# Ten weight buffers instead of two, six output buffers instead of two, three-fold buffers between the engines of the output stage, and ScalarE's output copy one step later

## The chip, the cores and the metric

The kernel runs on one core of one Trainium2 chip. The metric is device time in microseconds (us), lower is better. In this kernel each engine runs its own program, in which it waits for semaphores that the others raise: TensorE (matmul and transpose, with results in the memory called PSUM), VectorE, ScalarE, and the DMA queues, mostly fed by the Sync engine. In the views of the profile PE is TensorE, PEld its weight loads, DVE VectorE, ACT ScalarE and POOL GpSimd; L306 is line 306 of the kernel. "Landing" is the moment at which a DMA's data have arrived.

## The reference, cut to what matters

```python
# x: (8, 5696, 128) f32, h: (5696, 128); D = 128 channels, S = 5696 positions, batch 8
y = irfft(rfft(x, 2*S) * rfft(h, 2*S))[:, :S]         # causal long convolution, per channel
Y = rfft(y)[:, :64]                                    # the first 64 modes
Y = Y_r@w_r - Y_i@w_i + 1j*(Y_r@w_i + Y_i@w_r)         # per mode a 128 x 128 complex mix
u = y + irfft(Y)
out = u + maximum(u @ w_ch, 0)
```

w_r and w_i are 64 x 128 x 128 f32 each, 8.4 MB together; the output is 23.3 MB.

## The kernel before

The kernel works in stages: h and x are transposed and cast; then the *channel loop* multiplies, for each of 128 channels, a Toeplitz band (1440 KB, loaded as G[i], four buffers) by x; then a forward DFT on TensorE (90 matmuls), VectorE's two copies of its result out of PSUM (called XM), the mix, an inverse transform folded into the *output stage*. Two parts matter here.

The weight load. Sixteen chunks of 512 KB (8 modes each), preceded by the small w_ch (chunk 0), come in f32 through two staging buffers and are cast to f16 in turn by VectorE (even chunks) and ScalarE (odd ones):

```python
# Sync engine, after the channel loop's loads (cut)
for k, (kind, c) in enumerate(wchunks_s):
    if k >= NWST:                                   # NWST = 2
        sp.wait_ge(s_wc, k - NWST + 1)              # the chunk two before has been cast
    sp.dma_start(WST[k % NWST] ..., wsrc).then_inc(s_wl[k % NWST], 16)
# VectorE (even k) and ScalarE (odd k)
    wait_ge(s_wl[k % NWST], 16 * (k // NWST + 1)); wait_ge(s_wc, k)
    copy(wdst[:, m0 * D:(m0 + WMB) * D], WST[k % NWST][:, 0:WMB * D]).then_inc(s_wc, 1)
```

The output stage. It has 90 groups of four 128 x 128 tiles. For each group g: A (TensorE, 8 matmuls: u transposed, in PSUM), e1 (ScalarE copies it to uT), B (TensorE, u @ w_ch), d1 (VectorE: max and add, into oT), C (TensorE, 4 transposes back), e2 (the copy into the f32 output buffer ost, VectorE for even g and ScalarE for odd g), then the output DMA.

```python
# TensorE
for step in range(NG + 2):                          # NG = 90
    if step < NG:              stageA(step)
    if 1 <= step <= NG:        stageB(step - 1)
    if 2 <= step <= NG + 1:    stageC(step - 2)
# ScalarE
def emit_e2_act(gg):
    uu = gg % 2
    act.wait_ge(s_po, gg + 1)                       # C(gg) is done
    if gg >= 2:
        act.wait_ge(s_od[uu], 16 * (gg // 2))       # the DMA out of this ost has landed
    act.copy(ost[uu][:, :], pb16[6 + uu][:, 0:GB * P]).then_inc(s_e2a, 1)
for g in range(NG + 1):
    if g < NG:
        ...                                         # waits
        act.copy(uT_sb[ui][:, :], pb[2 + ui][:, 0:GB * P]).then_inc(s_e1, 1)
    if g >= 1 and (g - 1) % 2 == 1:
        emit_e2_act(g - 1)
# VectorE: d1(g), then e2(g-1) if g-1 is even
```

Of the kernel before, what the change touches and what calls it, by code (L numbers as in the profile page):

```python
# [4 lines left out]
P = 128  # L5
DT16 = mybir.dt.float16
DT32 = mybir.dt.float32
# [5 lines left out]
def bass_long_conv_fft__then__afno_spectral_mix_kernel(  # L13
    nc, x, h, moe_w_r, moe_w_i, moe_w_ch, out
):
    B, S, D = x.shape
# [12 lines left out]
    NGB = 4  # L29
    GB = min(4, B)  # L30
# [14 lines left out]
    WMB = 1  # L45
# [5 lines left out]
    NWLD_BASES = 1  # L51
    NWC_TOTAL = 1 + 2 * NWCH

    i16_np = np.eye(P, dtype=np.float16)
# [6 lines left out]
    for m in range(M):  # L61
# [19 lines left out]
    g_bytes = GC * 2  # L81
    ph2_bytes = (2 * HALF + B * P * 3 + 512 * 2) * 2 + 2 * GB * P * 2 * 2 + 2 * GB * P * 4
    xst_bytes = B * D * 4
# [18 lines left out]
    uT_sb = [nc.alloc_sbuf_tensor_at(f"uT_sb{i}", [P, GB * P], DT16, offset=p2 + i * GB * P * 2)  # L102
             for i in range(2)]
    p2 += 2 * GB * P * 2
    oT_sb = [nc.alloc_sbuf_tensor_at(f"oT_sb{i}", [P, GB * P], DT16, offset=p2 + i * GB * P * 2)
             for i in range(2)]
    p2 += 2 * GB * P * 2
    ost = [nc.alloc_sbuf_tensor_at(f"ost{i}", [P, GB * P], DT32, offset=p2 + i * GB * P * 4)
           for i in range(2)]
    p2 += 2 * GB * P * 4  # L110
    assert p2 <= r2_addr + r2_bytes, (p2 - r2_addr, r2_bytes)
# [16 lines left out]
    WST = [nc.alloc_sbuf_tensor_at(f"WST{i}", [P, WMB * D], DT32, offset=ib_addr + i * wst_bytes)  # L128
           for i in range(NWST)]
    WCH16 = nc.alloc_sbuf_tensor("WCH16", [P, D], DT16)  # L130
    I16 = nc.alloc_sbuf_tensor("I16", [P, P], DT16)
# [3 lines left out]
    pb = [nc.alloc_psum_tensor(f"pb{i}", [P, 512], DT32) for i in range(8)]  # L135
    pb16 = [pb[i][:, :].bitcast(DT16) for i in range(8)]

    def sem(name):
        return nc.alloc_semaphore(name)
# [16 lines left out]
    s_wld = sem("s_wld")  # L156
    s_wl = [sem("s_wl0"), sem("s_wl1")]
    s_wc = sem("s_wc")
# [15 lines left out]
    s_e2a = sem("s_e2a")  # L174
    s_od = [sem("s_od0"), sem("s_od1")]

    with nc.Block() as block:
        @block.sync
        def _(sp):
# [36 lines left out]
            for k, (kind, c) in enumerate(wchunks_s):  # L216
                if k >= NWST:
                    sp.wait_ge(s_wc, k - NWST + 1)
                if kind == "wch":
                    sp.dma_start(WST[k % NWST][:, 0:D], moe_w_ch).then_inc(s_wl[k % NWST], 16)  # L220
                else:
                    w = moe_w_r if kind == "wr" else moe_w_i
                    m0 = c * WMB
                    wsrc = bass.AP(w.tensor, w.offset + m0 * D * D, [[D, P], [D * D, WMB], [1, D]])
                    wdstap = bass.AP(WST[k % NWST], 0, [[WMB * D, P], [D, WMB], [1, D]])
                    sp.dma_start(wdstap, wsrc).then_inc(s_wl[k % NWST], 16)
            for g in range(NG):
                q = g // NGRP_Q
                b0 = (g % NGRP_Q) * GB
                rows = P if q < NQ - 1 else TAIL  # L230
                if g % 2 == 0:
                    sp.wait_ge(s_e2d, g // 2 + 1)
                else:
                    sp.wait_ge(s_e2a, (g - 1) // 2 + 1)
                osrc = bass.AP(ost[g % 2], 0, [[GB * P, rows], [P, GB], [1, P]])
                odst = bass.AP(out.tensor, out.offset + b0 * S * D + q * P * D,
                               [[D, rows], [S * D, GB], [1, D]])
                sp.dma_start(odst, osrc).then_inc(s_od[g % 2], 16)
            sp.wait_ge(s_od[0], 16 * ((NG + 1) // 2))
            if NG >= 2:  # L240
                sp.wait_ge(s_od[1], 16 * (NG // 2))

# [15 lines left out]
        def _(act):  # L258
# [31 lines left out]
            for k, (kind, c) in enumerate(wchunks_a):  # L290
                if k % 2 != 1:
                    continue
                act.wait_ge(s_wl[k % NWST], 16 * (k // NWST + 1))
                act.wait_ge(s_wc, k)
                wdst = WR16 if kind == "wr" else WI16
                m0 = c * WMB
                act.copy(wdst[:, m0 * D:(m0 + WMB) * D], WST[k % NWST][:, 0:WMB * D]).then_inc(s_wc, 1)  # L297
            act.wait_ge(s_xtp, B)
            act.wait_ge(s_xt, 1)
            act.activation(XTn_sb[:, :], pb16[6][:, 0:B * P], ACT_COPY, scale=-1.0).then_inc(s_xt, 1)  # L300
            def emit_e2_act(gg):
                uu = gg % 2
                act.wait_ge(s_po, gg + 1)
                if gg >= 2:
                    act.wait_ge(s_od[uu], 16 * (gg // 2))
                act.copy(ost[uu][:, :], pb16[6 + uu][:, 0:GB * P]).then_inc(s_e2a, 1)  # L306
            for g in range(NG + 1):
                if g < NG:
                    ui = g % 2
                    act.wait_ge(s_put, g + 1)  # L310
                    if g >= 2:
                        act.wait_ge(s_prt, g - 1)
                        act.wait_ge(s_d1, g - 1)
                    act.copy(uT_sb[ui][:, :], pb[2 + ui][:, 0:GB * P]).then_inc(s_e1, 1)  # L314
                if g >= 1 and (g - 1) % 2 == 1:
                    emit_e2_act(g - 1)

        @block.vector
        def _(dve):
# [28 lines left out]
            for k, (kind, c) in enumerate(wchunks):  # L348
                if k % 2 != 0:
                    continue  # L350
                dve.wait_ge(s_wl[k % NWST], 16 * (k // NWST + 1))
                if k >= 1:
                    dve.wait_ge(s_wc, k)
                if kind == "wch":
                    dve.tensor_copy(WCH16[:, :], WST[k % NWST][:, 0:D]).then_inc(s_wc, 1)  # L355
                else:
                    wdst = WR16 if kind == "wr" else WI16
                    m0 = c * WMB
                    dve.tensor_copy(wdst[:, m0 * D:(m0 + WMB) * D], WST[k % NWST][:, 0:WMB * D]).then_inc(s_wc, 1)  # L359
            dve.wait_ge(s_dft, 2)  # L360
# [16 lines left out]
            def emit_e2_dve(gg):  # L377
                uu = gg % 2
                dve.wait_ge(s_po, gg + 1)
                if gg >= 2:  # L380
                    dve.wait_ge(s_od[uu], 16 * (gg // 2))
                dve.tensor_copy(ost[uu][:, :], pb16[6 + uu][:, 0:GB * P]).then_inc(s_e2d, 1)  # L382
            for g in range(NG + 1):
                if g < NG:
                    ui = g % 2
                    dve.wait_ge(s_prt, g + 1)
                    dve.wait_ge(s_e1, g + 1)
                    if g >= 2:
                        dve.wait_ge(s_po, g - 1)
                    dve.scalar_tensor_tensor(oT_sb[ui][:, :], pb[4 + ui][:, 0:GB * P], 0.0,  # L390
                                             uT_sb[ui][:, :], MAXOP, ADDOP).then_inc(s_d1, 1)
                if g >= 1 and (g - 1) % 2 == 0:
                    emit_e2_dve(g - 1)

        @block.tensor
        def _(pe):
# [75 lines left out]
            def stageA(g):  # L472
                ui = g % 2
                q = g // NGRP_Q
                b0 = (g % NGRP_Q) * GB
                if g >= 2:
                    pe.wait_ge(s_e1, g - 1)
                last = None
                for j in range(GB):
                    b = b0 + j  # L480
                    ao = bass.AP(AXC, q * B + b, [[NTOT, P], [NCOL, P]])
                    cols = pb[2 + ui][:, j * P:(j + 1) * P]
                    pe.matmul(cols, ao, I16[:, :], start=True, stop=False)  # L483
                    last = pe.matmul(cols, C_sb[:, b * P:(b + 1) * P], IB_sb[:, q * P:(q + 1) * P],  # L484
                                     start=False, stop=True)
                last.then_inc(s_put, 1)

            def stageB(g):
                ui = g % 2
                if g >= 2:  # L490
                    pe.wait_ge(s_d1, g - 1)
                pe.wait_ge(s_e1, g + 1)
                pe.matmul(pb[4 + ui][:, 0:GB * P], WCH16[:, :], uT_sb[ui][:, :],  # L493
                          start=True, stop=True).then_inc(s_prt, 1)

            def stageC(g):
                ui = g % 2
                if g >= 2:
                    if g % 2 == 0:
                        pe.wait_ge(s_e2d, (g - 2) // 2 + 1)  # L500
                    else:
                        pe.wait_ge(s_e2a, (g - 3) // 2 + 1)
                pe.wait_ge(s_d1, g + 1)
                last = None
                for j in range(GB):
                    last = pe.transpose(pb16[6 + ui][:, j * P:(j + 1) * P],  # L506
                                        oT_sb[ui][:, j * P:(j + 1) * P], I16[:, :])
                last.then_inc(s_po, 1)
# [38 lines left out]
```

## Time and profile before

828.48 us, the median of 4 runs (827.27 to 829.39). The first rows of the page's picture of the span, in 40 slices of about 20.7 us, each digit the busy tenths of a slice, with the clock granted to TensorE below:

```profile
PE   0777775899999999999999999999997076666674
...
DVE  0555553011111111111111111111111235655564
...
PEclk9755555899999999999999999999999559999997
```

TensorE is full through the long middle (the channel loop and the DFT). Then comes one slice at 0, and after it a last part where nothing is full. The windows view of the kernel before puts numbers on it. Its columns are the stretch, its length, the busy us of TensorE, its weight loads, VectorE, ScalarE and GpSimd, the granted clock, the busy share of the DMA engines and GB/s:

```profile
148.00:600.00 452.00, 451.88 (x5566) 391.28 (x5567) 65.49 (x123) 0.00 (x0) 0.00 (x0) 0.99 1.00 406
...
616.00:635.00 19.00, 19.00 (x90) 8.61 (x88) 2.08 (x3) 4.10 (x4) 0.00 (x0) 1.00 0.69 193
636.00:656.00 20.00, 0.00 (x0) 0.00 (x0) 2.63 (x4) 4.18 (x4) 0.00 (x0) 0.54 0.72 204
...
690.00:740.00 50.00, 32.90 (x413) 25.35 (x411) 30.62 (x48) 23.46 (x46) 0.00 (x0) 1.00 0.57 165
```

From 636 to 656 TensorE does nothing. In the output stage (690 to 740) TensorE is busy 66%, VectorE 61%, ScalarE 47%, DMA 0.57. The chain of waits (the chain of work that ended last, in order of time: start, length, what) tells what each stretch waits for. First in the weight load:

```profile
615.86 4.33 DMA WST<-in_moe_w_r_dram
620.22 0.70 DVE WR L359
620.94 4.38 DMA WST<-in_moe_w_r_dram
625.35 0.70 DVE WR L359
...
```

A landing, a cast, a landing: with two buffers, the next load of a buffer starts only after its cast. The copies of XM stand behind the casts in VectorE's program, so TensorE's next work waits for the last cast (656.29). Then in the output stage, in the same view:

```profile
740.01 0.59 ACT ost L306
...
740.62 2.58 DMA out_dram<-ost
...
743.27 0.59 ACT ost L306
...
743.88 2.46 DMA out_dram<-ost
...
```

ScalarE's copy into its one ost buffer, the DMA out of it until it has landed, the next copy: once per pair of groups. The waits view of 690 to 740 us (engine and line, what it waited for, us in total, times, longest) names the same wait first:

```profile
ACT ost L306 <- DMA out_dram<-ost: 25.1, 15, 2.1
DVE oT_sb L390 <- PE pb L493: 20.3, 16, 1.7
PE pb L493 <- ACT uT_sb L314: 18.1, 16, 1.6
```

### The profile page before, as it was taken

The numbers are of one execution on the slowest core, as the hardware profiler recorded it, in microseconds if no ns is written. First come the engines' busy times: TensorE is split into PE (matmuls) and PEld (weight loads), VectorE is DVE, ScalarE is ACT, GpSimd is POOL, SyncE is SP. The second block draws the span as 40 slices with busy tenths as digits, with TensorE's granted clock in tenths as the row PEclk, the third lists the DMA queues.
The fourth block names the chain that finished last, engine by engine and source line by source line (L and its number), as shares of the span: only waits on it lengthen the run. The fifth ranks groups of instructions, "written<-read, shape, count | busy, mean of one in ns | idle before, by whom it ended". The sixth has DMA issues, their size and how long they took to land.

```text
span 827.0 us, 16480 instructions
## 1 busy us (share of the span) xinstructions
PE 689.0 (83%) x7435; PEld 514.3 (62%) x7435; DVE 232.3 (28%) x395; ACT 113.7 (14%) x213; POOL 2.5 (0%) x9
## 2 busy tenths in 40 slices
PE   0777775899999999999999999999997076666674
PEld 0200000688888888888888888888873064545453
DVE  0555553011111111111111111111111235655564
ACT  1322221000000000000000000000002215454443
POOL 0000000000000000000000000000000000000000
PEclk9755555899999999999999999999999559999997
DMA  9877774999999999999999999999956615555554
GB/s 264 228 211 222 218 216 156 367 393 419 401 418 400 409 409 410 403 407 406 413 404 411 407 406 411 404 414 399 416 215 193 193 54 163 169 156 172 156 156 141
DMA packets 130949, 252.43 MB, mean 305 GB/s; under 512 B 4864, under 2 KB 112704, under 8 KB 114112
## 3 DMA queue, kind: packets, MB, share of 16 engines
q1 hardware_dynamic: 121232, 152.55, 53.2%
q10 hardware_dynamic: 9360, 95.88, 28.6%
q0 software_dynamic: 288, 2.95, 1.0%
q8 instruction: 59, 0.97, 0.4%
q14 instruction: 10, 0.08, 0.0%
HBM read 226.53 MB, written 24.84 MB: 304 GB/s over the span
## 4 chain that ended last, share of the span: by engine, by line
PE 66%; DMA 21%; DVE 5%; issue 4%; ACT 3%; SPq 0%; ACTq 0%; DVEq 0%
PE pb L431 56%; DMA out_dram<-ost 13%; PE pb L419 6%; DVE X L335 4%; ACT ost L306 3%; DMA WST<-in_moe_w_r_dram 2%; DMA WST<-in_moe_w_i_dram 2%; DMA hnat<-in_h_dram 2%; PE pb L406 1%; DMA G<-hT16scr 1%; DMA hT16scr<-hTsb 1%; PE pb L493 0%; DVE WR L359 0%; DVE WI L359 0%; PE pb L483 0%
## 5 line engine op out<-in xcount | busy, mean ns | idle before, releaser
L431 PE MATMUL pb<-AXC,G 128*128 128x360 f16 (+44 forms) x5760 | 467.0, 243 | 9.2 <-DMA G<-hT16scr 9.2
L431 PEld LDWEIGHTS pb<-AXC,G 128*128 128x128 f16 x5760 | 404.4, 98 | 73.4 <-issue 10.8
L346 DVE CAST AXC<-pb 128x360 f16<-128x360 f32 x128 | 68.2, 532 | 408.8 <-PE pb L431 408.8
L419 PE MATMUL pb<-X,J 128*128 128x512 f16 x90 | 84.7, 1029 | 26.5 <-DVE X L335 23.4
L390 DVE SCALAR_TENSOR_TENSOR oT_sb<-pb,uT_sb 128x512 f16<-128x512 f32 x90 | 61.8, 686 | 58.3 <-PE pb L493 58.3
L493 PE MATMUL pb<-uT_sb,WCH 128*128 128x512 f16 x90 | 35.5, 395 | 50.0 <-ACT uT_sb L314 50.0
L419 PEld LDWEIGHTS pb<-X,J 128*128 128x128 f16 x90 | 9.2, 103 | 100.5 <-DVE X L335 93.0
L297 ACT CAST WR<-WST 128x1024 f16<-128x1024 f32 x4 | 4.2, 1045 | 490.2 <-DVE WCH L355 476.4
L483 PE MATMUL pb<-I,AXC 128*128 128x128 f16 x360 | 53.9, 230 | 2.6 <-DVE C_sb L376 2.6
L484 PE MATMUL pb<-IB_sb,C_sb 128*128 128x128 f16 x360 | 53.5, 226 | 0.0
L314 ACT CAST uT_sb<-pb 128x512 f16<-128x512 f32 x90 | 48.9, 598 | 14.5 <-PE pb L484 14.5
L483 PEld LDWEIGHTS pb<-I,AXC 128*128 128x128 f16 x360 | 44.9, 141 | 2.8 <-DVE C_sb L376 2.8
L342 DVE CAST AXC<-pb 128x512 f16<-128x512 f32 x45 | 31.1, 692 | 52.9 <-PE pb L419 52.9
L493 PEld LDWEIGHTS pb<-uT_sb,WCH 128*128 128x128 f16 x90 | 8.9, 99 | 56.6 <-DVE oT_sb L390 49.3
L484 PEld LDWEIGHTS pb<-IB_sb,C_sb 128*128 128x128 f16 x360 | 38.0, 106 | 0.3 <-issue 0.3
L277 ACT CAST AXC<-pb 128x512 f16<-128x512 f32 x45 | 26.3, 585 | 85.2 <-PE pb L419 78.8
L306 ACT CAST ost<-pb 128x512 f32<-128x512 f16 x45 | 26.3, 585 | 77.7 <-DMA out_dram<-ost 69.6
L506 PE MATMUL pb<-I,oT_sb 128*128 128x128 f16 x360 | 36.0, 224 | 0.4 <-DVE oT_sb L390 0.4
L506 PEld LDWEIGHTS pb<-I,oT_sb 128*128 128x128 f16 x360 | 25.3, 99 | 16.2 <-issue 13.5
L382 DVE CAST ost<-pb 128x512 f32<-128x512 f16 x45 | 31.0, 689 | 3.5 <-DMA out_dram<-ost 2.8
L335 DVE CAST X<-XST 128x1024 f16<-128x1024 f32 x45 | 30.7, 683 | 0.0
L406 PE MATMUL pb<-I,hnat 128*128 128x128 f32 (+1 forms) x45 | 9.0, 358 | 18.7 <-DMA hnat<-in_h_dram 18.7
(45 smaller groups left out, 129.7 us busy)
## 6 DMA issues: line engine op xcount, KB each, us to landing
G<-hT16scr SPq DMA_DIRECT2D x64, 1440.0 KB, 9.0
G<-hT16scr ACTq DMA_DIRECT2D x64, 1440.0 KB, 8.9
XST<-in_x_dram SPq DMA_DIRECT2D x44, 512.0 KB, 4.6
out_dram<-ost SPq DMA_DIRECT2D x88, 256.0 KB, 2.4
WST<-in_moe_w_r_dram SPq DMA_DIRECT2D x8, 512.0 KB, 4.5
WST<-in_moe_w_i_dram SPq DMA_DIRECT2D x8, 512.0 KB, 4.2
hT16scr<-hTsb ACTq DMA_DIRECT2D x1, 1472.0 KB, 6.4
FB_sb<-cFB POOLq DMA_DIRECT2D x1, 1440.0 KB, 6.8
```

The source lines that it names most:

```text
L306: act.copy(ost[uu][:, :], pb16[6 + uu][:, 0:GB * P]).then_inc(s_e2a, 1)
L314: act.copy(uT_sb[ui][:, :], pb[2 + ui][:, 0:GB * P]).then_inc(s_e1, 1)
L335: dve.tensor_copy(X16[qi][:, :], XST[qi][:, :]).then_inc(s_cast, 1)
L342: dve.tensor_copy(dst, pb[g % 2][:, 0:HCOLS]).then_inc(s_jevd, 1)
L346: dve.tensor_copy(AXC[:, d * NCOL:(d + 1) * NCOL], pb[d % 4][:, 0:NCOL]).then_inc(s_cev, 1)
L390: dve.scalar_tensor_tensor(oT_sb[ui][:, :], pb[4 + ui][:, 0:GB * P], 0.0, uT_sb[ui][:, :], MAXOP, ADDOP).then_inc(s_d1, 1)
L419: pe.matmul(pb[g % 2][:, 0:HCOLS], J16[:, :], moving, start=True, stop=True).then_inc(s_j, 1)
L431: ins = pe.matmul(pb[d % 4][:, B * l:NCOL], G[i][:, l * P:(l + 1) * P], AXC[:, d * NCOL:d * NCOL + ncols], start=(l == 0), stop=(l == NQ - 1))
L483: pe.matmul(cols, ao, I16[:, :], start=True, stop=False)
L484: last = pe.matmul(cols, C_sb[:, b * P:(b + 1) * P], IB_sb[:, q * P:(q + 1) * P], start=False, stop=True)
L493: pe.matmul(pb[4 + ui][:, 0:GB * P], WCH16[:, :], uT_sb[ui][:, :], start=True, stop=True).then_inc(s_prt, 1)
L506: last = pe.transpose(pb16[6 + ui][:, j * P:(j + 1) * P], oT_sb[ui][:, j * P:(j + 1) * P], I16[:, :])
```

## The change

The intent is to hide the weight load and to keep the output stage from waiting for its own output. Chunks 2 to 9 get buffers in the channel loop's G buffers, free as the last four channels finish. The output stage gets six ost buffers (NO) and three of uT, oT and their PSUM banks (ND). ScalarE's ost copy moves one step later in its program. The diff, cut to its core:

```diff
+    ND = 3
+    NO = 6
@@ weight staging
+    # chunk buffers 2..9: two in each G buffer, free once the last channel of that buffer is done
+    WST += [nc.alloc_sbuf_tensor_at(f"WSTG{i}", [P, WMB * D], DT32,
+                                    offset=r2_addr + (i // 2) * g_bytes + (i % 2) * wst_bytes)
+            for i in range(2 * NGB)]
+    NWB = len(WST)
@@ Sync engine
-                if k >= NWST:
-                    sp.wait_ge(s_wc, k - NWST + 1)
+                if k >= NWB:
+                    sp.wait_ge(s_wc, k - NWB + 1)
+                elif k >= NWST:
+                    sp.wait_ge(s_cd, D - NGB + 1 + (k - NWST) // 2)
@@ ScalarE
             def emit_e2_act(gg):
-                uu = gg % 2
+                uu = gg % NO
                 act.wait_ge(s_po, gg + 1)
-                if gg >= 2:
-                    act.wait_ge(s_od[uu], 16 * (gg // 2))
+                if gg >= NO:
+                    act.wait_ge(s_od[uu], 16 * (gg // NO))
-            for g in range(NG + 1):
+            for g in range(NG + 2):
                 if g < NG:
-                    ui = g % 2
+                    ui = g % ND
...
-                if g >= 1 and (g - 1) % 2 == 1:
-                    emit_e2_act(g - 1)
+                if g >= 2 and (g - 2) % 2 == 1:
+                    emit_e2_act(g - 2)
```

Left out: the same renaming of indices (2 to ND, NO or NWB) on the other engines; one added wait of VectorE for the last weight cast, because the buffers that follow lie over the new staging; and a constant that nothing uses.

More of the change, by code (lines that the diff above doesn't have):

```diff
@@ L52, in bass_long_conv_fft__then__afno_spectral_mix_kernel @@
     NWC_TOTAL = 1 + 2 * NWCH
+    WLOAD_START_D = max(NGB, D - 4 * (NWC_TOTAL + 3))
     i16_np = np.eye(P, dtype=np.float16)
@@ L81, in bass_long_conv_fft__then__afno_spectral_mix_kernel @@
     g_bytes = GC * 2
-    ph2_bytes = (2 * HALF + B * P * 3 + 512 * 2) * 2 + 2 * GB * P * 2 * 2 + 2 * GB * P * 4
+    ND = 3
+    NO = 6
+    ph2_bytes = (2 * HALF + B * P * 3 + 512 * 2) * 2 + 2 * ND * GB * P * 2 + NO * GB * P * 4
     xst_bytes = B * D * 4
@@ L102, in bass_long_conv_fft__then__afno_spectral_mix_kernel @@
     uT_sb = [nc.alloc_sbuf_tensor_at(f"uT_sb{i}", [P, GB * P], DT16, offset=p2 + i * GB * P * 2)
-             for i in range(2)]
-    p2 += 2 * GB * P * 2
+             for i in range(ND)]
+    p2 += ND * GB * P * 2
     oT_sb = [nc.alloc_sbuf_tensor_at(f"oT_sb{i}", [P, GB * P], DT16, offset=p2 + i * GB * P * 2)
-             for i in range(2)]
-    p2 += 2 * GB * P * 2
+             for i in range(ND)]
+    p2 += ND * GB * P * 2
     ost = [nc.alloc_sbuf_tensor_at(f"ost{i}", [P, GB * P], DT32, offset=p2 + i * GB * P * 4)
-           for i in range(2)]
-    p2 += 2 * GB * P * 4
+           for i in range(NO)]
+    p2 += NO * GB * P * 4
     assert p2 <= r2_addr + r2_bytes, (p2 - r2_addr, r2_bytes)
@@ L136, in bass_long_conv_fft__then__afno_spectral_mix_kernel @@
     pb16 = [pb[i][:, :].bitcast(DT16) for i in range(8)]
+    pb_uT = [pb[i] for i in range(ND)]
+    pb_rT = [pb[ND + i] for i in range(ND)]
+    pb_o16 = [pb16[6][:, 0:GB * P], pb16[7][:, 0:GB * P]]
     def sem(name):
@@ L156, in bass_long_conv_fft__then__afno_spectral_mix_kernel @@
     s_wld = sem("s_wld")
-    s_wl = [sem("s_wl0"), sem("s_wl1")]
+    s_wl = [sem(f"s_wl{i}") for i in range(NWB)]
     s_wc = sem("s_wc")
@@ L174, in bass_long_conv_fft__then__afno_spectral_mix_kernel @@
     s_e2a = sem("s_e2a")
-    s_od = [sem("s_od0"), sem("s_od1")]
+    s_od = [sem(f"s_od{i}") for i in range(NO)]
     with nc.Block() as block:
@@ L216, in _ @@
             for k, (kind, c) in enumerate(wchunks_s):
-                if k >= NWST:
-                    sp.wait_ge(s_wc, k - NWST + 1)
+                if k >= NWB:
+                    sp.wait_ge(s_wc, k - NWB + 1)
+                elif k >= NWST:
+                    sp.wait_ge(s_cd, D - NGB + 1 + (k - NWST) // 2)
                 if kind == "wch":
-                    sp.dma_start(WST[k % NWST][:, 0:D], moe_w_ch).then_inc(s_wl[k % NWST], 16)
+                    sp.dma_start(WST[k % NWB][:, 0:D], moe_w_ch).then_inc(s_wl[k % NWB], 16)
                 else:
@@ L224, in _ @@
                     wsrc = bass.AP(w.tensor, w.offset + m0 * D * D, [[D, P], [D * D, WMB], [1, D]])
-                    wdstap = bass.AP(WST[k % NWST], 0, [[WMB * D, P], [D, WMB], [1, D]])
-                    sp.dma_start(wdstap, wsrc).then_inc(s_wl[k % NWST], 16)
+                    wdstap = bass.AP(WST[k % NWB], 0, [[WMB * D, P], [D, WMB], [1, D]])
+                    sp.dma_start(wdstap, wsrc).then_inc(s_wl[k % NWB], 16)
             for g in range(NG):
@@ L234, in _ @@
                     sp.wait_ge(s_e2a, (g - 1) // 2 + 1)
-                osrc = bass.AP(ost[g % 2], 0, [[GB * P, rows], [P, GB], [1, P]])
+                osrc = bass.AP(ost[g % NO], 0, [[GB * P, rows], [P, GB], [1, P]])
                 odst = bass.AP(out.tensor, out.offset + b0 * S * D + q * P * D,
                                [[D, rows], [S * D, GB], [1, D]])
-                sp.dma_start(odst, osrc).then_inc(s_od[g % 2], 16)
-            sp.wait_ge(s_od[0], 16 * ((NG + 1) // 2))
-            if NG >= 2:
-                sp.wait_ge(s_od[1], 16 * (NG // 2))
+                sp.dma_start(odst, osrc).then_inc(s_od[g % NO], 16)
+            for i in range(NO):
+                cnt = len([g for g in range(NG) if g % NO == i])
+                if cnt > 0:
+                    sp.wait_ge(s_od[i], 16 * cnt)
         @block.gpsimd
@@ L292, in _ @@
                     continue
-                act.wait_ge(s_wl[k % NWST], 16 * (k // NWST + 1))
+                act.wait_ge(s_wl[k % NWB], 16 * (k // NWB + 1))
                 act.wait_ge(s_wc, k)
@@ L296, in _ @@
                 m0 = c * WMB
-                act.copy(wdst[:, m0 * D:(m0 + WMB) * D], WST[k % NWST][:, 0:WMB * D]).then_inc(s_wc, 1)
+                act.copy(wdst[:, m0 * D:(m0 + WMB) * D], WST[k % NWB][:, 0:WMB * D]).then_inc(s_wc, 1)
             act.wait_ge(s_xtp, B)
@@ L301, in emit_e2_act @@
             def emit_e2_act(gg):
-                uu = gg % 2
+                uu = gg % NO
                 act.wait_ge(s_po, gg + 1)
-                if gg >= 2:
-                    act.wait_ge(s_od[uu], 16 * (gg // 2))
-                act.copy(ost[uu][:, :], pb16[6 + uu][:, 0:GB * P]).then_inc(s_e2a, 1)
-            for g in range(NG + 1):
+                if gg >= NO:
+                    act.wait_ge(s_od[uu], 16 * (gg // NO))
+                act.copy(ost[uu][:, :], pb_o16[gg % 2]).then_inc(s_e2a, 1)
+            for g in range(NG + 2):
                 if g < NG:
-                    ui = g % 2
+                    ui = g % ND
                     act.wait_ge(s_put, g + 1)
-                    if g >= 2:
-                        act.wait_ge(s_prt, g - 1)
-                        act.wait_ge(s_d1, g - 1)
-                    act.copy(uT_sb[ui][:, :], pb[2 + ui][:, 0:GB * P]).then_inc(s_e1, 1)
-                if g >= 1 and (g - 1) % 2 == 1:
-                    emit_e2_act(g - 1)
+                    if g >= ND:
+                        act.wait_ge(s_prt, g - ND + 1)
+                        act.wait_ge(s_d1, g - ND + 1)
+                    act.copy(uT_sb[ui][:, :], pb_uT[ui][:, 0:GB * P]).then_inc(s_e1, 1)
+                if g >= 2 and (g - 2) % 2 == 1:
+                    emit_e2_act(g - 2)
         @block.vector
@@ L350, in _ @@
                     continue
-                dve.wait_ge(s_wl[k % NWST], 16 * (k // NWST + 1))
+                dve.wait_ge(s_wl[k % NWB], 16 * (k // NWB + 1))
                 if k >= 1:
@@ L354, in _ @@
                 if kind == "wch":
-                    dve.tensor_copy(WCH16[:, :], WST[k % NWST][:, 0:D]).then_inc(s_wc, 1)
+                    dve.tensor_copy(WCH16[:, :], WST[k % NWB][:, 0:D]).then_inc(s_wc, 1)
                 else:
@@ L358, in _ @@
                     m0 = c * WMB
-                    dve.tensor_copy(wdst[:, m0 * D:(m0 + WMB) * D], WST[k % NWST][:, 0:WMB * D]).then_inc(s_wc, 1)
+                    dve.tensor_copy(wdst[:, m0 * D:(m0 + WMB) * D], WST[k % NWB][:, 0:WMB * D]).then_inc(s_wc, 1)
+            dve.wait_ge(s_wc, NWC_TOTAL)
             dve.wait_ge(s_dft, 2)
@@ L377, in emit_e2_dve @@
             def emit_e2_dve(gg):
-                uu = gg % 2
+                uu = gg % NO
                 dve.wait_ge(s_po, gg + 1)
-                if gg >= 2:
-                    dve.wait_ge(s_od[uu], 16 * (gg // 2))
-                dve.tensor_copy(ost[uu][:, :], pb16[6 + uu][:, 0:GB * P]).then_inc(s_e2d, 1)
+                if gg >= NO:
+                    dve.wait_ge(s_od[uu], 16 * (gg // NO))
+                dve.tensor_copy(ost[uu][:, :], pb_o16[gg % 2]).then_inc(s_e2d, 1)
             for g in range(NG + 1):
                 if g < NG:
-                    ui = g % 2
+                    ui = g % ND
                     dve.wait_ge(s_prt, g + 1)
                     dve.wait_ge(s_e1, g + 1)
-                    if g >= 2:
-                        dve.wait_ge(s_po, g - 1)
-                    dve.scalar_tensor_tensor(oT_sb[ui][:, :], pb[4 + ui][:, 0:GB * P], 0.0,
+                    if g >= ND:
+                        dve.wait_ge(s_po, g - ND + 1)
+                    dve.scalar_tensor_tensor(oT_sb[ui][:, :], pb_rT[ui][:, 0:GB * P], 0.0,
                                              uT_sb[ui][:, :], MAXOP, ADDOP).then_inc(s_d1, 1)
@@ L472, in stageA @@
             def stageA(g):
-                ui = g % 2
+                ui = g % ND
                 q = g // NGRP_Q
                 b0 = (g % NGRP_Q) * GB
-                if g >= 2:
-                    pe.wait_ge(s_e1, g - 1)
+                if g >= ND:
+                    pe.wait_ge(s_e1, g - ND + 1)
                 last = None
@@ L481, in stageA @@
                     ao = bass.AP(AXC, q * B + b, [[NTOT, P], [NCOL, P]])
-                    cols = pb[2 + ui][:, j * P:(j + 1) * P]
+                    cols = pb_uT[ui][:, j * P:(j + 1) * P]
                     pe.matmul(cols, ao, I16[:, :], start=True, stop=False)
@@ L488, in stageB @@
             def stageB(g):
-                ui = g % 2
-                if g >= 2:
-                    pe.wait_ge(s_d1, g - 1)
+                ui = g % ND
+                if g >= ND:
+                    pe.wait_ge(s_d1, g - ND + 1)
                 pe.wait_ge(s_e1, g + 1)
-                pe.matmul(pb[4 + ui][:, 0:GB * P], WCH16[:, :], uT_sb[ui][:, :],
+                pe.matmul(pb_rT[ui][:, 0:GB * P], WCH16[:, :], uT_sb[ui][:, :],
                           start=True, stop=True).then_inc(s_prt, 1)
             def stageC(g):
-                ui = g % 2
+                ui = g % ND
+                og = g % 2
                 if g >= 2:
@@ L505, in stageC @@
                 for j in range(GB):
-                    last = pe.transpose(pb16[6 + ui][:, j * P:(j + 1) * P],
+                    last = pe.transpose(pb_o16[og][:, j * P:(j + 1) * P],
                                         oT_sb[ui][:, j * P:(j + 1) * P], I16[:, :])
```

## The prediction

> What bounds the kernel now. The page's engine row has TensorE busy 83% of 827.0 us, but the stages have different limits. In the windows view: 148 to 615 us is the channel loop, TensorE full and DMA at 1.00; 616 to 635 is the forward DFT, TensorE full; 636 to 656 TensorE does nothing; from 673.6 to 827 (the output stage, 90 groups) TensorE is busy 65%, VectorE 60%, ScalarE 48%, DMA 0.56. None is full there.
>
> Idle 1, the weight load. The chain of waits shows alternating "DMA WST" (4.25 to 4.54 us) and a VectorE cast (0.70) from 615.9 to 656.3: only two chunk buffers, so each 512 KB pair waits for casts and for the landing. The DFT ended at 635.4, so some 21 us are exposed.
>
> Idle 2, the output stage. The chain is 94% output DMA (2.3 to 3.3 us) plus ScalarE's ost copy (0.59), once per pair of groups: ScalarE may not refill its one buffer until its DMA has landed. Period 3.16 us per pair in mid-stage.
>
> What the change does. (a) Eight more weight buffers in the G region; chunks 2 to 9 start as channels 124 to 127 finish (from 604 us), so about 8 of 16 chunks are there or in flight when casting starts at 615.6. The rest, some 4.7 MB, at about 300 GB/s (the first 15 us of the trace: 305 GB/s with DMA full) takes 16 us, landing near 632. Casts cost 0.7 (VectorE) and 1.04 (ScalarE), strictly in turn: 15 us in all. Both end before the DFT at 635.4, so the intermediate copies start about 21 us earlier. Cost: the early chunks share the DMA engines with the last G loads, 0 to 2 us. (b) Six ost buffers, so the wait for the landing leaves the chain; ScalarE's ost copy comes a step later. (c) Three uT/rT PSUM and SBUF buffers. Instruction counts barely change.
>
> The new bound of the output stage, per pair of groups: VectorE three operations, start to start 0.60 when back to back (timeline): 1.82. TensorE: 0.47 + 0.21 + 0.22 per group: 1.80. ScalarE three at about 0.50: 1.5. DMA 512 KB at 291 GB/s (163 GB/s at share 0.56): 1.80. Three nearly equal limits, coupled in order, won't overlap perfectly. Following the semaphores by these durations, I estimate 2.0 to 2.1 per pair (the same arithmetic gives 3.26 for the kernel before, measured 3.16). 45 pairs and the ends: about 99 us instead of 153.5, saving 52 to 54.
>
> TensorE's clock. The windows view has it at 0.50 from 640 to 676, after the idle stretch. The Trainium skill, "TensorE: Matmul & The Clock Gate", Part 1, says activity releases the throttle and idleness restores it; the trace agrees. With the idle stretch gone the first groups may run warm, 1 or 2 us, not more: the 256 small matmuls start every 26.5 ns.
>
> Sum: 828.5 - 21 - 53 + 1 = about 755 us, range 744 to 772. Chances: faster 0.97, same 0.02, slower 0.01.
>
> Right if: the chain no longer has "DMA WST" nor a landing-bound "out_dram" in mid-stage; the DFT is followed within 1 us by the XM copies near 636; output groups come at 1.0 to 1.1 us; VectorE is over 85% busy and DMA over 0.8 there, with 230 to 250 GB/s; no ScalarE wait for out_dram.
>
> Wrong if: many 512-byte writes in flight sustain less than 291 GB/s (at 240 the stage takes 97 us from DMA alone, more with waits); TensorE, ScalarE and VectorE lock step at 2.4 or more per pair; early weight loads starve the last two channels; or the weights still end after the DFT.

## The result, and the profile after

756.44 us, the median of 8 runs (754.93 to 757.81). The ratio to the kernel before is 0.9129, with a 95% interval of 0.912 to 0.9139. Here and below a ratio is the mean time of one kernel's fast runs over that of the other's fast runs of the same rounds, so it is not quite the ratio of the medians. The result is correct.

The windows view of the changed kernel, with the columns as before:

```profile
148.00:600.00 452.00, 451.68 (x5571) 391.19 (x5572) 65.48 (x123) 0.00 (x0) 0.00 (x0) 1.00 1.00 406
600.00:615.00 15.00, 14.93 (x194) 12.92 (x191) 2.17 (x5) 0.00 (x0) 0.00 (x0) 1.00 1.03 348
616.00:635.00 19.00, 19.00 (x89) 8.53 (x87) 4.86 (x7) 7.03 (x7) 0.00 (x0) 1.00 1.16 291
636.00:654.00 18.00, 8.95 (x280) 8.54 (x280) 6.53 (x12) 1.85 (x2) 0.53 (x1) 0.63 0.24 86
660.00:700.00 40.00, 38.88 (x519) 31.39 (x518) 37.18 (x60) 30.55 (x60) 0.00 (x0) 1.00 0.90 259
```

The channel loop is as it was. From 600 us on the DMA engines carry weights next to the last G loads, and in the DFT they are full (a share over 1, 291 GB/s against 193 before). In the output stage TensorE is busy 97%, VectorE 93%, ScalarE 76%, DMA 0.90 at 259 GB/s. VectorE's timeline (start, busy us, what, and in brackets the idle time before it and what ended it) shows the end of the weights:

```profile
620.72 0.69 DVE L373 CAST WR<-WSTG 128x1024 f16<-128x1024 f32 x1 [1.23 <-ACT WR L311]
623.42 0.69 DVE L373 CAST WR<-WSTG 128x1024 f16<-128x1024 f32 x1 [2.01 <-DMA WSTG<-in_moe_w_r_dram]
...
633.99 0.69 DVE L373 CAST WI<-WSTG 128x1024 f16<-128x1024 f32 x1 [2.88 <-DMA WSTG<-in_moe_w_i_dram]
637.30 0.69 DVE L373 CAST WI<-WSTG 128x1024 f16<-128x1024 f32 x1 [2.62 <-DMA WSTG<-in_moe_w_i_dram]
638.03 0.69 DVE L376 CAST XM_sb<-pb 128x512 f16<-128x512 f32 x1
...
```

Until 621 us the casts pass the turn to each other at once; from 623 on each waits for a landing. The last one is cast at 637.3, and XM follows at 638.03. TensorE had finished the DFT at about 635.2 and waited:

```profile
PE pb L446 <- DMA G<-hT16scr: 9.6, 1, 9.6
PE pb L463 <- DVE XM_sb L377: 4.2, 1, 4.2
```

(In the kernel before, XM's buffer doesn't lie over the weight staging, so only the order of VectorE's program held it behind the casts. From the first copy of XM to the mix takes 4.0 us in the changed kernel, 638.03 to 642.00; so copying XM ahead of the last casts could have saved about that much at most in the kernel before, an estimate. It was not tried.)

The 9.6 us wait for G is the start of the channel loop (9.2 before), so the early weights did not starve the last channels. In the output stage, 690 to 740 us before is answered by this waits view of the changed kernel:

```profile
ACT uT_sb L328 <- PE pb L499: 11.6, 25, 0.6
PEld pb L522 <- issue: 9.0, 32, 0.4
DVE oT_sb L405 <- PE pb L508: 2.9, 13, 0.2
```

No wait for a landing is left in mid-stage. VectorE's timeline gives the pace: the same pattern comes back after two pairs of groups.

```profile
735.03 0.69 DVE L405 SCALAR_TENSOR_TENSOR oT_sb<-pb,uT_sb 128x512 f16<-128x512 f32 x1 [0.23 <-PE pb L508]
735.64 0.68 DVE L397 CAST ost<-pb 128x512 f32<-128x512 f16 x1
736.24 1.43 DVE L405 SCALAR_TENSOR_TENSOR oT_sb<-pb,uT_sb 128x512 f16<-128x512 f32 x2
...
739.09 0.69 DVE L405 SCALAR_TENSOR_TENSOR oT_sb<-pb,uT_sb 128x512 f16<-128x512 f32 x1 [0.22 <-PE pb L508]
739.70 0.68 DVE L397 CAST ost<-pb 128x512 f32<-128x512 f16 x1
740.29 1.44 DVE L405 SCALAR_TENSOR_TENSOR oT_sb<-pb,uT_sb 128x512 f16<-128x512 f32 x2
...
743.15 0.69 DVE L405 SCALAR_TENSOR_TENSOR oT_sb<-pb,uT_sb 128x512 f16<-128x512 f32 x1 [0.22 <-PE pb L508]
...
```

From 735.03 to 739.09 to 743.15 is 4.06 us for four groups, 2.03 us per pair, against about 3.2 before (3.26 between the two copies shown there). The paces per pair below are VectorE's ost copies, start to start, averaged over 660 to 745 us.

Where the 74.9 us between the two traces (827.0 and 752.1) came from: the XM copies start at 638.03 instead of 656.90, which is 18.9; from there to the first output matmul it takes 16.3 us instead of 16.7 (654.31 and 673.56 in the timelines); the output stage from there to the end takes 97.8 instead of 153.4, which is 55.6. The medians differ by less, 72.0 us: the profiled run of the changed kernel took 753.96 us, 2.5 below its median (the kernel before: 828.76 against 828.48). Where these 2.5 us lie is not known, so the three parts are good to 2 or 3 us.

### The profile page after: what moved, and what is told of

The parts are those of the page before. It is cut to its first block, busy times and chain, and to the rows that moved or that the text cites. A ratio compares the mean times of both kernels' runs of the same rounds, so it can differ in the third digit from the quotient of the medians.

```text
span 752.1 us, 16477 instructions
## 1 busy us (share of the span) xinstructions
PE 679.3 (90%) x7435; PEld 509.6 (68%) x7435; DVE 229.4 (31%) x395; ACT 113.7 (15%) x213; POOL 2.5 (0%) x9
## 4 chain that ended last, share of the span: by engine, by line
PE 82%; DMA 7%; DVE 5%; issue 4%; ACT 0%; SPq 0%; DVEq 0%; ACTq 0%
PE pb L446 62%; PE pb L434 6%; DVE X L349 4%; PE pb L522 3%; PE pb L498 3%; PE pb L499 3%; PE pb L508 3%; DMA hnat<-in_h_dram 2%; DMA WSTG<-in_moe_w_i_dram 2%; DMA G<-hT16scr 1%; PE pb L421 1%; DMA WSTG<-in_moe_w_r_dram 1%; DMA hT16scr<-hTsb 1%; DVE AXC L356 0%; DVE oT_sb L405 0%
## 5 line engine op out<-in xcount | busy, mean ns | idle before, releaser
L311 ACT CAST WR<-WST 128x1024 f16<-128x1024 f32 x1 | 1.0, 1044 | 476.4 <-DVE WCH L369 476.4
L328 ACT CAST uT_sb<-pb 128x512 f16<-128x512 f32 x90 | 53.5, 595 | 35.1 <-PE pb L499 34.7
L522 PEld LDWEIGHTS pb<-I,oT_sb 128*128 128x128 f16 x360 | 23.0, 96 | 20.4 <-issue 17.1
L421 PEld LDWEIGHTS pb<-I,hnat 128*128 128x128 f32 (+1 forms) x45 | 6.5, 160 | 20.9 <-issue 18.6
```

Source lines behind the costliest of these rows:

```text
L328: act.copy(uT_sb[ui][:, :], pb_uT[ui][:, 0:GB * P]).then_inc(s_e1, 1)
L522: last = pe.transpose(pb_o16[og][:, j * P:(j + 1) * P], oT_sb[ui][:, j * P:(j + 1) * P], I16[:, :])
```

## The experiments

Twelve kernels ran, in three sets. Kernels of a set ran on the same chip and shared the runs of the kernel before (828.36, 827.59 and 828.07 us in the three sets).

### First set: which part of the change does it

The output part has three ingredients that the diff changes together: more ost buffers, third buffers between the engines, and ScalarE's copy one step later. Theory A was that the order and the ost buffers do it, theory B that the third buffers do.

**two_banks**, the changed kernel with

```diff
-    ND = 3
+    ND = 2
```

> The changed kernel with two instead of three uT, rT and oT buffers; the rest of the change stays. Theory A (what frees the output stage is that ScalarE's ost copy comes one step later in its own program, plus the ost buffers; the third buffers idle): unchanged, 756 us, 2.03 us per pair of groups. Theory B (the third buffers are what lets the engines overlap): back towards 2.87 us per pair, which is my walk through the waits for the kernel with six ost buffers and the old order, so 45 x 0.84 = 38 us more, about 794 us.

Measured: 756.02 us (755.35 to 756.81), as with three. The third buffers do nothing here; theory B falls.

**act_early**, the changed kernel with ScalarE's old order:

```diff
-            for g in range(NG + 2):
+            for g in range(NG + 1):
...
-                if g >= 2 and (g - 2) % 2 == 1:
-                    emit_e2_act(g - 2)
+                if g >= 1 and (g - 1) % 2 == 1:
+                    emit_e2_act(g - 1)
```

> The changed kernel with ScalarE's ost copy of group g-1 (as before) in place of g-2; three buffers and six ost buffers stay. Theory A (order on ScalarE): ScalarE stands waiting for the transposes of g-1 while the uT copy of the next group, already due, queues behind it; 2.87 us per pair, about 794 us, and the waits view shows ScalarE's ost copy waiting for TensorE. Theory B (third buffers): unchanged at 756 us.

Measured: 792.25 us (791.22 to 794.26), 2.89 us per pair. Two views show where the time goes. ScalarE's timeline:

```profile
699.72 0.59 ACT L320 CAST ost<-pb 128x512 f32<-128x512 f16 x1 [1.33 <-PE pb L522]
700.21 1.08 ACT L328 CAST uT_sb<-pb 128x512 f16<-128x512 f32 x2
702.61 0.59 ACT L320 CAST ost<-pb 128x512 f32<-128x512 f16 x1 [1.33 <-PE pb L522]
...
```

and the waits of 690 to 740 us:

```profile
ACT ost L320 <- PE pb L522: 22.5, 17, 1.3
...
PE pb L508 <- ACT uT_sb L328: 13.5, 17, 0.8
```

ScalarE stands 1.33 us in front of the ost copy because the transposes of that group are not done; then it does that copy and two uT copies back to back. The first of those two had been due earlier, and TensorE's B waits for it 0.8 us. In ScalarE's program the copy that isn't ready holds up the ready one behind it. Moving it one step later removes this, with no more buffers.

**two_ost**, the changed kernel with

```diff
-    NO = 6
+    NO = 2
```

> The changed kernel with two ost buffers. Both theories: the copy waits for the landing again, 3.1 to 3.2 us per pair, so about 805 to 810 us; if it lies below 790 us the landing was not the limit before.

Measured: 806.42 us (806.02 to 807.45), 3.18 us per pair. The wait for the landing is back, in the waits of 660 to 740 us:

```profile
DVE ost L397 <- DMA out_dram<-ost: 32.4, 25, 1.6
ACT ost L320 <- DMA out_dram<-ost: 28.8, 25, 1.4
```

**weights_only**, the kernel before with only the weight part (the changed kernel with ND and NO at 2 and ScalarE's old order).

> The kernel before with only the eight more weight buffers. If the two halves of the change add up, the 18.9 us by which the XM copies came earlier in the trace of the changed kernel remain: 828.5 - 19 = 809.5 us. Rival: the earlier weights pay in part by something else (a warmer TensorE clock in the output stage, or a slower one), then it is off that by over 2 us.

Measured: 808.96 us (807.28 to 810.65), 19.4 us faster than the 828.36 of its set. So the weight part is worth about 19 us with the old output stage too (18.9 in the trace of the changed kernel); the rival, a side effect on the output stage of over 2 us, doesn't show.

All four are from one set, so the output part can be taken apart from 808.96 us, the kernel with the weight part only: six ost buffers (and the idle third buffers) with the old order give 16.7 us (792.25), the new order with two ost buffers 2.5 us (806.42), both together with two banks 52.9 us (756.02). Neither ingredient alone gives a third of what both give: with the old order ScalarE stands waiting for the transposes, with two ost buffers for the landing. Not run: the old order or two ost buffers with ND = 2, so the third buffers are shown idle only where both other ingredients are in, and the output part without the weight part.

### Second set: what sets the new pace, and can the weights move

**half_out**, the changed kernel with half of each output buffer moved. Its output is wrong, which doesn't matter for the time.

```diff
-                osrc = bass.AP(ost[g % NO], 0, [[GB * P, rows], [P, GB], [1, P]])
+                osrc = bass.AP(ost[g % NO], 0, [[GB * P, rows], [P, GB // 2], [1, P]])
```

(and the same for the target)

> The changed kernel, whose output DMAs move half of each buffer (the result is wrong on purpose). The output stage of the changed kernel shows DMA at 0.90 to 0.92 of its engines' time. Theory A (engines coupled in order set 2.03 us per pair, DMA is near its limit but not the limit): 755 us, at most 1 us off for a shorter last landing. Theory B (DMA sets the pace): well below, at the 1.8 to 1.9 us per pair that TensorE or VectorE alone would allow, 748 us or less.

Measured: 755.07 us (754.6 to 756.37), 2.04 us per pair. Its windows view:

```profile
660.00:700.00 40.00, 38.92 (x512) 31.12 (x511) 36.86 (x60) 31.06 (x60) 0.00 (x0) 1.00 0.44 126
```

With half the bytes the pace is the same, so DMA at 0.90 did not set it.

**late_c**, the changed kernel with TensorE's transposes one step later, and ScalarE's copy with them (VectorE's copy keeps its place):

```diff
-            for step in range(NG + 2):
+            for step in range(NG + 3):
...
-                if 2 <= step <= NG + 1:
-                    stageC(step - 2)
+                if 3 <= step <= NG + 2:
+                    stageC(step - 3)
@@ ScalarE
-                if g >= 2 and (g - 2) % 2 == 1:
-                    emit_e2_act(g - 2)
+                if g >= 3 and (g - 3) % 2 == 1:
+                    emit_e2_act(g - 3)
```

> The changed kernel with TensorE's output transposes one step later still (group g-3 after group g's first matmuls), and ScalarE's ost copy with them; this is where the third buffers are needed. Theory A (TensorE stands waiting for VectorE's result of one step earlier): the wait goes, and the pace comes to what DMA can do, 1.86 us per pair by 262 GB/s at share 0.92, so 45 x 0.17 = 7.5 us less, about 749 us. Theory B (DMA or VectorE already sets 2.03): unchanged, 756 us.

Measured: 748.99 us (747.46 to 750.29), ratio to before 0.9053 (0.9033 to 0.9074), 1.86 us per pair. Its windows view:

```profile
700.00:735.00 35.00, 35.00 (x492) 30.51 (x491) 34.92 (x58) 29.74 (x57) 0.00 (x0) 1.00 1.00 282
```

TensorE and VectorE are now busy throughout. In the waits of 690 to 740 us, TensorE's weight loads for C at line 522, 9.0 us in 32 waits in the changed kernel (shown above; the view can't name the cause and calls it issue), are gone: 0.4 us remain in 690 to 735. In the changed kernel's timeline each C that waits starts 0.14 us after a d1 ends (for instance 702.45 after 701.63 + 0.68), so I read those waits as waits for d1. The gain, 6.1 us against half_out of the same set and 7.5 against the changed kernel's own median, fits that.

**early_w**, the changed kernel with all weight chunks loaded during the channel loop, one per six channels through the two old buffers, and cast by ScalarE:

```diff
                 sp.dma_start(G[i][:, :], gsrc).then_inc(s_gr[i], 16)
+                if d >= 4 and (d - 4) % 6 == 0 and (d - 4) // 6 < NWC_TOTAL:
+                    load_chunk((d - 4) // 6)
@@ ScalarE, after its own G loads
+                if d >= 9 and (d - 9) % 6 == 0 and (d - 9) // 6 < NWC_TOTAL:
+                    cast_chunk((d - 9) // 6)
```

> The changed kernel with all weight chunks loaded and cast during the channel loop, one chunk per six channels through the two old chunk buffers, cast on ScalarE, which is idle there. If the DMA engines have room beside the G loads (406 GB/s, share 1.00): the XM copies follow the DFT at 636 instead of 638, so 2 to 3 us less, about 753.5 us, and perhaps a few more if TensorE then keeps its clock. If share 1.00 means what it says: 8.5 MB at 406 GB/s is 21 us more of channel loop, about 774 us.

Measured: 783.34 us (782.47 to 785.59), 27 us slower than the changed kernel. The share of 1.00 in the channel loop meant what it said. TensorE's waits in 148 to 640 us (9.5 of them are the start of the loop, as before):

```profile
PE pb L441 <- DMA G<-hT16scr: 34.9, 25, 9.5
```

The obvious rival is the lesson of act_early: the new loads and casts stand in front of G loads in the programs of the Sync engine and of ScalarE. But in 148 to 650 us Sync never waits for a cast, ScalarE's casts never wait for a landing (waits views), and in a windows view of five stretches from 148 to 640 us the DMA share is 0.98 to 1.01: the DMA engines were full. The last channel's result is copied at 649.31 instead of 614.97, 34.3 us later. I had expected 21 us, the weights' bytes at 406 GB/s. But weights come in rows of 512 bytes, at about 300 GB/s (1.75 us per chunk in the changed kernel): 16 x 1.75 = 28 us, and the 1.47 MB of the inverse base, which now also falls in the loop, some 4 us at 406 GB/s. That sum, 32, is an estimate. The total grew less than the loop: XM follows the last channel after 20.3 us instead of 23.1, and the profiled run of early_w was slower than its median (785.59 against 783.34 us), that of the changed kernel faster (753.96 against 756.44).

**both**, late_c and early_w together.

> late_c and early_w together. If both do what theory A and room on the DMA engines say, they add: about 746 us. If early_w loses, the sum of the two differences is expected all the same.

Measured: 775.38 us (773.59 to 777.17), 8.0 us below early_w; the later transposes are worth as much here as alone.

### Third set: the limits of the better version, and a best one

**late_c_half_out**, late_c with half of each output buffer moved, edited as in half_out. Its output is wrong, which doesn't matter for the time.

> The version with the later transposes (749 us, TensorE, VectorE and DMA all at 0.95 to 1.00 of their time in its output stage, about 1.86 us per pair of groups), with half of each output buffer moved (the result is wrong on purpose). If DMA is now the limit: the compute engines' own pace shows, 1.80 to 1.82 us per pair by my sums, so 1 to 3 us less, about 747 us. If VectorE and TensorE are: unchanged, 749 us.

Measured: 747.78 us (745.52 to 748.62). The total can't tell: its ratio, 0.9027 (0.9011 to 0.9044), overlaps that of late_c. The traces can: 1.862 us per pair against 1.864 (VectorE's ost copies, start to start over the stage). Its windows view:

```profile
700.00:735.00 35.00, 35.00 (x491) 30.36 (x489) 34.96 (x57) 29.33 (x57) 0.00 (x0) 1.00 0.49 143
```

The DMA share fell from 1.00 to 0.49 and the pace stayed. So late_c isn't limited by DMA either, although I had derived its 1.86 us from the DMA rate. The number was right and its reason wrong: VectorE's three operations take 0.61 and two in 1.24 us start to start (timeline), which is 1.86, and TensorE is busy throughout too, though the ends of its records are modelled. Which of the two holds the other was not separated.

**late_c_two_banks**, late_c with ND = 2.

> The version with the later transposes with two instead of three uT, rT and oT buffers. Here the third buffers should be needed, because VectorE's result must wait for the transposes that empty its buffer, which now come a step later: 2.69 us per pair by my walk through the waits, 45 x 0.83 = 37 us more, about 786 us. If the third buffers are of no use here either: 749 us.

Measured: 787.47 us (787.04 to 788.5), 2.78 us per pair. With the later transposes the third buffers are needed. In the change as given they were room that nothing used. In the trace VectorE stands 25.6 us (29 times, 660 to 740 us) in front of its ost copy, waiting for the transposes, one instruction before the max-and-add at which the expectation had put the wait, and TensorE's B 21.5 us for uT. Which of these waits closes the ring was not taken apart.

**three_ost**, the changed kernel with NO = 3.

> The changed kernel with three ost buffers in place of six. A buffer is in use for its copy (0.6), the issue and landing (2.8) and comes up again every 3 groups (3 x 1.01 = 3.05 us), so it just falls short: 2.1 us per pair, 756 + 4 = about 760 us. If landings are longer under load, more: up to 775.

Measured: 771.23 us (770.55 to 773.52), 2.40 us per pair: a miss of 11 us against 760, within the "up to 775" for longer landings. The waits of 660 to 740 us:

```profile
ACT ost L320 <- DMA out_dram<-ost: 12.4, 19, 2.0
...
DVE ost L397 <- DMA out_dram<-ost: 7.4, 12, 1.5
PE pb L508 <- ACT uT_sb L328: 6.6, 8, 1.8
...
ACT ost L320 <- PE pb L522: 3.0, 8, 1.1
```

My sum took one landing time, 2.8 us. In the trace landings run from 2.3 to 4.2 us, and a late one stops the copy and what stands behind it: the view has 6.6 us of waits by TensorE for uT, against 0.3 us, once, in the changed kernel's output stage. That the spread of the landings is the cause was not tried by itself.

**best**, late_c with four of the sixteen weight chunks loaded and cast in the first matmul stage, where the DMA engines are at 0.72 (40 to 137 us, windows view of the kernel before) and ScalarE is mostly idle:

```diff
                 sp.dma_start(xdst, xsrc).then_inc(s_xd[i], 16)
+                if q >= 8 and q % 8 == 0 and q // 8 <= NEARLY:      # NEARLY = 4
+                    j = q // 8 - 1
+                    ...                                              # load w_i chunk NWCH - NEARLY + j into WST[j % 2]
@@ ScalarE, after its copy of x block q
+                if q >= 12 and q % 8 == 4 and q // 8 <= NEARLY:
+                    ...                                              # cast it into WI16
```

> The version with the later transposes, and four of the sixteen weight chunks loaded and cast already in the first matmul stage (40 to 137 us), where the DMA engines are at 0.72 and ScalarE is mostly idle. The weights in the forward DFT are then 12 chunks; at 1.75 us each they end some 7 us earlier, before the DFT, so the XM copies come 2.0 to 2.6 us earlier: about 746.5 us. Rival: the extra loads disturb the first stage, each by up to 1 to 2 us, and eat the gain: 748 to 752.

Measured: 745.55 us (744.56 to 745.8), ratio to before 0.9003 (0.8989 to 0.9016), correct. XM now starts 20.3 us after the last channel's copy (634.51 and 614.22) instead of 23.1 (638.03 and 614.97), 2.8 us less, and VectorE waits there for the end of the DFT (4.47 us) and no longer for a cast. It is the fastest of all kernels here.

## Why the prediction was right

The total of 755 us met 756.44, and the range of 744 to 772 held it. Its terms, one by one, against the trace:

- The weights: predicted 21 us, measured 18.9. The step that was off is "about 8 of 16 chunks are there or in flight when casting starts at 615.6. The rest, some 4.7 MB ... landing near 632". In flight isn't landed. After 615.6 the chunks land 1.75 us apart until 637.3, which makes some 12 still to come, not 9: until about 609 us the last G loads had the DMA engines too. The rate, 300 GB/s, was right. So "Both end before the DFT" was wrong, and the sign "the DFT is followed within 1 us by the XM copies" failed: XM came 2.8 us after the DFT, and TensorE waited 4.2 us in all. The chain of waits also still has weight landings. One of the prediction's own conditions for being wrong, "the weights still end after the DFT", thus came true; the total held because the weights came only 2 us late.
- The output stage: predicted about 99 us and 2.0 to 2.1 us per pair, measured 97.8 and 2.03. It holds because the durations were taken start to start from the trace (0.60 for VectorE though each record lasts 0.69) and the waits were followed in program order: the same arithmetic gave 2.87 for act_early (measured 2.89) and 2.69 for late_c_two_banks (2.78), but missed three_ost (2.1, measured 2.40). VectorE at 93%, DMA at 0.90 and the lack of a wait for out_dram came as said; 259 GB/s is a little over the 230 to 250 named.
- "Three nearly equal limits, coupled in order": the coupling was shown (half_out unchanged, late_c 6 to 7.5 us faster). DMA as one of the limits was not: with half the bytes nothing changed, twice.
- TensorE's clock: "the first groups may run warm, 1 or 2 us" did not come. From XM to the first output matmul 0.4 us were saved, and the clock from 646 to 654 is 0.50 in a windows view of 4 us steps.
- The prediction lists the third buffers as an ingredient and doesn't say which ingredient counts. two_banks and act_early show it: not the buffers, but the place of one copy in ScalarE's program, together with the ost buffers.

That the total came within 1.5 us is in part luck. By the traces the weights gave 2 us less than forecast, while the channels that did not starve (1 us), the output stage (55.6 against 53) and the stretch between (0.4) gave 4 us more: a saving of 74.9 against 73 in the sum. By the medians it is 72.0, because the profiled run was a quick one.

## What to carry to other kernels

Before adding buffers, look at what stands in front of the waiting instruction in its own engine's program: a copy that was issued one step too early cost 36 us here (act_early against the changed kernel), and the third buffers gave nothing until the order asked for them. Cost each ingredient alone and all together, since two waits in one loop hide each other: 16.7 and 2.5 us alone, 52.9 together. When a transfer is to hide beside another stage, count the bytes that have landed by then at the rate of their own row length, and test with half the bytes whether a full-looking DMA share is a limit at all.

## What the Trainium skill lacked or had wrong

- "DMA: Bandwidth & Descriptors", Specifications, gives 512 bytes or more as the transfer size for line rate. Here rows of 512 bytes moved at 291 GB/s (weights in the DFT, share 1.16) and 282 GB/s (output in late_c, share 1.00), while the G loads with rows of 11,520 bytes moved at 406 GB/s, share 1.00. At 512 bytes these runs don't reach the rate of the longer rows, so that line taken by itself promises too much. That the length of the rows is the whole cause was not tried: the G loads also read overlapping pieces of a small scratch.
- "Perfetto Trace Analysis", Identifying the Most-Contended Engine, calls occupancy misleading for the 16 DMA engines. The runs agree and give it a size: a share of 1.00 was no limit in late_c (half the bytes, share 0.49, 1.862 against 1.864 us per pair), and was one in the channel loop (early_w, 27 us slower). The section names HBM utilization instead, and by GB/s the two cases do differ (282 and 406). What it doesn't name is the direct test used here, to change the bytes and look at the pace.
- "Perfetto Trace Analysis", Optimization Strategy, says that consistent bubbles can mean too few buffers. The page calls ScalarE's queue strict FIFO where it treats single instructions, but doesn't name order inside one engine's program as a cause of bubbles: with all the buffers in place, act_early kept a wait of up to 1.33 us per pair on ScalarE and of 0.8 us on TensorE, and took 792.25 us.
- "TensorE: Matmul & The Clock Gate", Part 1, lets the clock follow how busy TensorE has been, but doesn't say how matmuls as small as these count. In early_w the clock fell to 0.50 while the records had TensorE busy 3.4 to 3.6 of every 4 us, with the mix's matmuls of 8 columns:

```profile
669.00:673.00 4.00, 1.21 (x11) 0.58 (x9) 2.52 (x5) 0.52 (x1) 0.00 (x0) 1.00 0.00 0
673.00:677.00 4.00, 3.44 (x130) 3.44 (x131) 0.00 (x0) 0.51 (x1) 0.00 (x0) 0.79 0.02 4
677.00:681.00 4.00, 3.57 (x132) 3.47 (x129) 0.33 (x1) 0.00 (x0) 0.00 (x0) 0.50 0.02 4
```

  Gaps of 1.45 and 1.90 us came just before the mix, so this fall alone could be their late effect. But in the changed kernel the mix fills 642 to 649 us without a gap (7.00 of 7.00 us busy) and the clock stays at 0.50, while in the output stage it goes from 0.50 (654 to 657) to 1.00 (658 to 662). So a busy row in the profile doesn't by itself raise the clock. What the gate counts, no run here shows.
